# VectorE and the sync engine held to program order from the third batch on, with v split and loaded a head sooner and evenly shared heads

## The chip, the cores and the metric

The kernel runs on one core of one Trainium2 chip. The time is device microseconds (us) of one launch. Before the change three runs took 1080.21, 1080.63 and 1082.72 us, median 1080.63 us.

The core's engines work side by side, each through its own list of instructions from first to last: PE (TensorE, the matmuls; PEld are its weight loads), DVE (VectorE), ACT (ScalarE), POOL (GpSimd) and SP (the sync engine, which issues all DMAs here). An instruction waits on semaphores for what it needs from the other engines, and while it waits, whatever stands behind it on its own engine waits too.

## The reference

Attention with a decay, then a feed-forward layer with a hard swish. Shapes: q, k, v (8 batches, 8 heads, 576, 64), f (8, 8, 576), w_in (512, 2048), w_out (2048, 512).

```python
scores = scale * np.matmul(q, k.transpose(0, 1, 3, 2))
log_f = np.log(np.clip(f, 0.0001, 1.0))
cum = np.cumsum(log_f, axis=-1)
decay = cum[:, :, :, None] - cum[:, :, None, :]
scores = np.where(causal, -1000000000.0, scores + decay)
scores = scores - np.max(scores, axis=-1, keepdims=True)
attn = np.exp(scores)
attn = attn / (np.sum(attn, axis=-1, keepdims=True) + 1e-09)
x = np.matmul(attn, v)      # to (4608 tokens, 512)
h = x @ w_in
g = h * np.clip(h + 3.0, 0.0, 6.0) / 6.0
out = g @ w_out
```

## The kernel before

**Two streams of work.** The list `VH` holds the attention steps v = 0 to 67: four of kind A and eight of kind B (batch 0, in pieces), then one of kind F for each head n = 8 to 63 (v = n + 4; batch b = n // 8, head h = n % 8). The feed-forward layer works on nine tiles of 512 tokens. Tile t has 16 h units (`h_unit`, 12 matmuls each, then clip and product) and four out units (`out_unit`, 48 matmuls each). A loop over `VH` writes one attention step per pass and calls `fill(1)` eight times in it. Each call adds a rate to a credit, and as long as the credit is at least 1 it takes the next piece of a feed-forward unit from the list `units` (an h unit is two pieces of 1.05, an out unit eight of 0.95, a tile 64 in all). From the third batch on the rate is 1.02, so 8.16 per head. When the eight heads of a batch are done, `done` puts that batch's tile into `units`; after the last batch two tiles are left.

**One head of kind F** (`rows`) goes through two halves. PE makes the scores of a half (tile `pn`, lines 608 and 611: 8 matmuls for half 0, 4 for half 1). DVE adds the mask and takes the row maximum (line 619, three chunks in half 0 and two in half 1) and makes the bias `nb` (line 625). ACT takes the exponential (line 631) and casts it to 16 bits into a `ring` buffer (line 645). DVE makes the low part (line 648, two per half) and POOL the rest (lines 654, 659). SP transposes the ring buffer into `pT` by DMA (line 666). A pass later PE multiplies with v (`av`, tile `pav`, 40 matmuls), and DVE normalizes (`rs`, `xf`, lines 727 to 729; every second head `xhl`, line 735). Every second head SP transposes the result into `xT`, the feed-forward input (`x_move`, line 755).

**One h unit**: PE fills a PSUM bank `ph` with 12 matmuls (lines 781 to 783). ACT makes `r` from it in two segments, one for each batch that the tile touches (line 791). DVE multiplies (line 794), and this is the last read of the bank; ACT casts to `gT` (line 795) and DVE makes the low part (line 796). `mm_tile` has three such banks in turn, so the unit after next but one cannot start before line 794 of this one is done.

**v of a batch**: `load_v` loads it into `vst` (lines 359, 360; called at h = 6 of the batch before). `v_scale` (h = 7) finds its largest value with two reductions on DVE (line 365), a matmul `pt_v` and some small steps. `v_split` (lines 396, 397) makes 16-bit high and low parts for a pair of heads, at h = 7 for the first pair and at h = 1, 3 and 5 for the others.

**What sets the order.** The program is written once in this loop, but the order on each engine is decided by a scheduler that plays the program on a model of the chip and lets each engine take what is ready there, earlier lines first. So the lists of the engines are not in the program's order. [...]

Of the kernel before, what the change touches and what calls it, by code (L numbers as in the profile page):

```python
# [20 lines left out]
def kernel(  # L21
# [10 lines left out]
    nc = tc.nc  # L32
# [3 lines left out]
    B = vS.shape[0]  # L36
    H = NHEAD // B
    NT, DM = out.shape
    DFF = w_in.shape[1]
    P = 128  # L40
    NCH = 5
    CR = [128, 128, 128, 128, 64]
    SP = NCH * P
    NPAIR = H // 2
    NCC = DM // P
    NFC = DFF // P
    TT = 512
# [9 lines left out]
    ps_m = ctx.enter_context(tc.tile_pool(name="ps_m", bufs=2, space=bass.MemoryType.PSUM))  # L57
    ps_t = ctx.enter_context(tc.tile_pool(name="ps_t", bufs=1, space=bass.MemoryType.PSUM))
# [23 lines left out]
    NQK, NL, NST = 3, 2, 3  # L82
    W_RATE = (8, 5, 4)
    H_COST = 1.05
    F_RATE = (0.6, 0.45, 1.02)
    PIN = 0
    PIN0 = 1
    LOW_W = 0
# [6 lines left out]
    QA = 256  # L95
    CA = QA // P
    VH = [("A", g) for g in range(NPAIR)] + [("B", n) for n in range(H)]
# [54 lines left out]
    SV, IV, UO, UX, A1 = 0, 8, 16, 24, 32  # L152
# [25 lines left out]


    def pow2_scale(pm, s_col, i_col, name):  # L180
        pool, tag = (ps_t, "tr") if SV < s_col < SV + B else (ps_m, "mm")
        pt = pool.tile([P, 512], F32, tag=tag, name=f"pt_{name}")
        nc.tensor.matmul(pt[:, 0:1], ones, pm, start=True, stop=True)
        yield
        e = p2.tile([P, 2], F32, tag="ee", name=f"e_{name}")
        nc.vector.tensor_scalar(e[:, 0:1], pt[:, 0:1], 2.0 ** -100, None, op0=ALU.max)
        ei = e.bitcast(I32)
        nc.vector.tensor_scalar(
            ei[:, 1:2], ei[:, 0:1], 24, 23, op0=ALU.logical_shift_right, op1=ALU.logical_shift_left
        )  # L190
        si = SC.bitcast(I32)
        nc.vector.tensor_scalar(
            si[:, s_col:s_col + 1], ei[:, 1:2], -1.0, float(204 << 23), op0=ALU.mult, op1=ALU.add
        )
        nc.vector.tensor_scalar(
            si[:, i_col:i_col + 1], ei[:, 1:2], 1.0, float(50 << 23), op0=ALU.mult, op1=ALU.add
        )
        yield

    def scol(c):  # L200
        return SC[:, c:c + 1]
# [160 lines left out]
    def v_scale(b):  # L362
        pm = p2.tile([P, 2], F32, tag="pm", name=f"vm{b}")
        for i, t in enumerate(v_parts(b)):
            nc.vector.tensor_reduce(
                pm[:, i:i + 1], t.rearrange("p c (h e) -> p (c h) e", e=D + 1)[:, :, 0:D],
                axis=AX.XY, op=ALU.max, apply_absolute_value=True,
            )
            yield
        nc.vector.tensor_tensor(pm, pm, pm, op=ALU.mult)  # L370
        nc.vector.tensor_tensor(pm[:, 0:1], pm[:, 0:1], pm[:, 1:2], op=ALU.max)
        yield from pow2_scale(pm[:, 0:1], SV + b, IV + b, f"v{b}")
# [15 lines left out]
    def v_split(g):  # L388
        b, hp = divmod(g, NPAIR)
        t = v16[:, g % NV16]  # L390
        if g < NPAIR + NV16:
            nc.vector.memset(t[:, :, :, D:D + 1], 1.0)
        for j in range(2):
            o = (2 * hp + j) * (D + 1)
            src = vst[:, :, o:o + D]
            nc.scalar.activation(t[:, :, j, 0:D], src, AF.Copy, scale=scol(SV + b))
            nc.vector.scalar_tensor_tensor(
                t[:, :, j, D + 1:VW], src, scol(SV + b), t[:, :, j, 0:D],
                op0=ALU.mult, op1=ALU.subtract,
            )  # L400

    def load_x(v):
        kind, n = VH[v]
        t = ST[v % NST]
        if kind == "A":
            nc.sync.dma_start(
                t[:, 0:2 * QA].rearrange("p (h s) -> p h s", h=2),
                qk[2 * n:2 * n + 2, :, 0:QA].rearrange("h p s -> p h s"),
            )
        else:  # L410
            nc.sync.dma_start(t, qk[n])

    def load_c(v):
        kind, n = VH[v]
        t = TK[v % NQK].bitcast(F32)[D:D + 2]
        if kind != "A":
            nc.sync.dma_start(t[:, 0:S], scr[n])
            if kind == "F":
                nc.sync.dma_start(TQ[v % NQK].bitcast(F32)[D + 2:D + 4, 0:S], scr[n])
        elif n >= 2:  # L420
            nc.sync.dma_start(
                t[:, 0:2 * QA].rearrange("r (h s) -> r h s", h=2),
                scr[2 * n:2 * n + 2, :, 0:QA].rearrange("h r s -> r h s"),
            )
        else:
            for h in range(2):
                d = nc.sync.dma_start(
                    t[:, h * QA:(h + 1) * QA], cs.bitcast(F32)[2 * n + h:2 * n + h + 1, :, 0:QA]
                )
            if PIN0:  # L430
                small.append(d.ins)
# [386 lines left out]
    def moe_tile(t, c0=0, c1=TT):  # L818
        for fc in range(NFC):
            j, new = divmod(fc, NFC // NG)  # L820
            if new == 0 and t < B and c0 == 0:
                while j not in w_in_done:
                    next(w_in_q, None)
                moe_scale_in(t, j)
            yield from h_unit(t, fc, c0, c1)
        if t == 0:
            for _ in wq:
                pass
        if t < B and c0 == 0:
            moe_scale_out(t)  # L830
        for s in range(c0 // P, c1 // P):
            yield from out_unit(t, s)
# [43 lines left out]

    units = []

    credit, rates = [0.0], [1.0]

    def w_step():
        with tc.high_priority(offset=-LOW_W):
            next(wq, None)

    def fill(k):
        credit[0] += k * rates[0]
        while credit[0] >= 1 and units:
            with tc.high_priority(offset=-LOW_M):
                r = next(units[0], 0)
            if r == 0:  # L890
                units.pop(0)
            else:
                credit[0] -= r
        credit[0] = min(credit[0], 1.0)

    def one(*a):
        yield from moe_tile(*a)

    def done(v):
        kind, n = VH[v]  # L900
        if kind == "A":
            if n == NPAIR - 1:
                units.append(one(0, 0, QA))
            return
        b, h = divmod(n, H)
        if h == H - 1:
            units.append(one(b, QA if b == 0 else 0, TT))
            if b == B - 1:
                units.append(one(B))

    prev = None
    pend_x = None
    vq = v_scale(0)
    for i, (kind, n) in enumerate(VH):
        b, h = divmod(n, H)
        if kind == "A":
            b = h = 0
        wn = W_RATE["ABF".index(kind)]
        rates[0] = F_RATE[0] if kind == "B" else F_RATE[min(b, 2)]
        ahead = i + 2 < NV  # L920
        if i + 3 < NV:
            load_x(i + 3)
        if ahead:
            load_c(i + 2)
        if b + 1 < B and h == 6:
            load_v(b + 1)
        if b and h % 2 == 1 and h < H - 1:
            v_split((n + 1) // 2)
        sg = rows(i) if kind == "F" else scores(i)
        front = ahead and VH[i + 2][0] != "F"  # L930
        next(sg)
        if i + 1 < NV:
            rests(i + 1)
        if ahead:
            parts(i + 2)
        fill(1)
        if b + 1 < B and h == 7:
            vq = v_scale(b + 1)
        next(vq, None)
        fill(1)  # L940
        ph = next(sg)
        if i + 1 < NV and VH[i + 1][0] != "F":
            max_rows(i + 1)
        for _ in range(wn // 2):
            w_step()
        fill(1)
        next(vq, None)
        next(sg, None)
        fill(1)
        if pend_x is not None:  # L950
            x_move(pend_x)
            done(pend_x)
            pend_x = None
        if front:
            natural(i + 2, 0)
        fill(1)
        if b + 1 < B and h == 7:
            for _ in vq:
                pass
            if b:  # L960
                v_split((n + 1) // 2)
        for _ in range(wn - wn // 2):
            w_step()
        next(sg, None)
        fill(1)
        if front:
            natural(i + 2, 1)
        fill(1)
        if prev is not None:
            av(*prev)  # L970
            if VH[prev[0]][0] == "A" or VH[prev[0]][1] % 2 == 1:
                pend_x = prev[0]
        if n == H:
            v_split(n // 2)
        fill(1)
        prev = (i, ph)
    rates[0] = 1.0
    av(*prev)
    fill(4)
    x_move(prev[0])  # L980
    done(prev[0])
    while units:
        fill(1)


# [34 lines left out]
```

## Time and profile before

| | |
|---|---|
| time, median of 3 runs | 1080.63 us |
| the profiled execution: its time, its span | 1083.28 us, 1081.5 us |
| PE busy | 1010.1 us (93%) |
| DVE busy | 719.7 us (67%) |
| ACT busy | 610.1 us (56%) |
| POOL busy | 413.1 us (38%) |
| mean granted TensorE clock | 0.982 |

A line of a view names engine, source line, operation and tiles (out<-in). "Idle before" is the engine's idle time just before an instruction, with what ended it. Heads take some 13 us each in the middle of the run: head n = 16 starts its scores at 236.9 us, n = 35 at 499.2, n = 36 at 511.8, n = 43 at 608.6 and n = 44 at 621.1. After the last head (879.5 us) only feed-forward work is left.

### The profile page before, as it was taken

How to read it: one execution, taken by the hardware profiler on the slowest of the kernel's cores; microseconds unless marked ns; L12 is line 12 of the kernel's file. 1: busy time of each engine (PE TensorE's matmuls, PEld its weight loads, DVE VectorE, ACT ScalarE, POOL GpSimd, SP SyncE). 2: the span in 40 equal slices, each digit the busy share in tenths (PEclk: the TensorE clock that was granted, in tenths of full speed). 3: DMA queues.
4: the chain of work that ended last, by engine and by line, in shares of the span. 5: the costliest groups of instructions: out<-in, count | busy, mean ns of one | idle time of the engine just before them, and what ended most of it. 6: DMA issues, size and time to landing. Idle time of an engine off the chain costs nothing.

```text
span 1081.5 us, 20281 instructions
## 1 busy us (share of the span) xinstructions
PE 1010.1 (93%) x7074; PEld 577.4 (53%) x7074; DVE 719.7 (67%) x1887; ACT 610.1 (56%) x1285; POOL 413.1 (38%) x505
## 2 busy tenths in 40 slices
PE   2799977988999999999999989999999999999998
PEld 2567854755555555555555545555555555444443
DVE  7869899876885688468865795689668841510520
ACT  4778656845764577356754674477447841621520
POOL 7344455335434445444544444454445420000000
PEclk9989989999999999999999999999999999999999
DMA  8866547767756666667576856675666651000001
GB/s 258 277 172 194 150 105 134 179 127 150 156 114 141 140 146 118 137 129 164 108 139 138 164 113 130 146 166 114 128 140 128 106 112 46 1 10 30 1 1 39
DMA packets 261650, 133.74 MB, mean 124 GB/s; under 512 B 229444, under 2 KB 231036, under 8 KB 261548
## 3 DMA queue, kind: packets, MB, share of 16 engines
q1 hardware_dynamic: 261548, 132.45, 54.7%
q8 instruction: 56, 0.92, 0.3%
q14 instruction: 46, 0.38, 0.1%
HBM read 47.93 MB, written 9.73 MB: 53 GB/s over the span
## 4 chain that ended last, share of the span: by engine, by line
PE 64%; DVE 12%; DMA 9%; issue 5%; ACT 5%; SPq 2%; POOL 2%; DVEq 0%; POOLq 0%; ACTq 0%
PE po L803 10%; PE po L804 10%; PE po L805 10%; PE ph L781 7%; PE ph L782 7%; PE ph L783 7%; DMA vst<-in_vS_dram 3%; PE pn L611 3%; PE pn L608 2%; DVE pp L619 2%; DVE ring L648 2%; DMA T<-TK 1%; DVE gT L796 1%; DMA w<-in_w_in_dram 1%; DVE r L794 1%
## 5 line engine op out<-in xcount | busy, mean ns | idle before, releaser
L781 PE MATMUL ph<-xT,w 128*128 128x512 f16 (+1 forms) x640 | 231.2, 363 | 14.5 <-DVE r L794 9.1
L782 PE MATMUL ph<-xT,w 128*128 128x512 f16 (+1 forms) x640 | 230.2, 363 | 0.0
L783 PE MATMUL ph<-xT,w 128*128 128x512 f16 (+1 forms) x640 | 230.0, 363 | 0.0
L631 ACT ACTIVATE pp<-pp,nb 128x192 f32<-128x192 f32 x280 | 138.5, 552 | 148.8 <-DVE nb L625 145.8
L804 PE MATMUL po<-w,gT 128*128 128x512 f16 x576 | 216.3, 381 | 6.1 <-DVE w L294 6.1
L805 PE MATMUL po<-w,gT 128*128 128x512 f16 x576 | 215.9, 381 | 0.0
L803 PE MATMUL po<-w,gT 128*128 128x512 f16 x576 | 213.6, 381 | 1.1 <-ACT o L814 0.8
L648 DVE TENSOR_TENSOR ring<-pp,ring 128x128 f16<-128x128 f32 (+2 forms) x216 | 131.5, 622 | 84.1 <-ACT ring L645 83.2
L791 ACT ACTIVATE r<-ph,bias_r,SC 128x256 f32<-128x256 f32 (+7 forms) x272 | 144.4, 570 | 28.6 <-PE ph L783 27.9
L794 DVE SCALAR_TENSOR_TENSOR r<-r,ph 128x512 f32<-128x512 f32 (+1 forms) x160 | 100.1, 627 | 88.9 <-ACT r L791 88.6
L458 POOL TENSOR_TENSOR T<-ST,T 64x576 fp32r<-64x576 f32 (+1 forms) x68 | 101.2, 1488 | 143.2 <-DMA T<-TK 133.4
L619 DVE CUSTOM_DVE_ANT_0 pp<-pn,W 128x192 f32<-128x192 f32 x280 | 122.9, 482 | 20.6 <-PE pn L611 16.6
L796 DVE TENSOR_TENSOR gT<-r,gT 128x512 f16<-128x512 f32 (+1 forms) x160 | 118.3, 743 | 27.4 <-ACT gT L795 26.6
L795 ACT CAST gT<-r 128x512 f16<-128x512 f32 (+1 forms) x160 | 91.8, 575 | 75.9 <-DVE r L794 75.8
L608 PE MATMUL pn<-TK,TQ 68*128 68x192 f32 x336 | 124.1, 383 | 5.8 <-issue 5.0
L611 PE MATMUL pn<-T,T 128*128 128x192 f32 x336 | 113.5, 368 | 4.3 <-POOL T L458 4.3
L645 ACT CAST ring<-pp 128x192 f16<-128x192 f32 x280 | 112.9, 452 | 0.0
L455 POOL TENSOR_TENSOR T<-ST,TQ 64x576 fp32r<-64x576 f32 (+2 forms) x68 | 97.6, 1435 | 24.8 <-PE pn L611 18.2
L654 POOL TENSOR_TENSOR ring<-pp,ring 128x128 f16<-128x128 f32 x96 | 61.5, 641 | 105.5 <-ACT ring L645 83.7
L782 PEld LDWEIGHTS <-w 128*128 128x128 f16 x640 | 62.7, 99 | 65.8 <-issue 20.9
L805 PEld LDWEIGHTS <-gT 128*128 128x128 f16 x576 | 56.8, 99 | 74.9 <-issue 13.7
L781 PEld LDWEIGHTS <-w 128*128 128x128 f16 x640 | 63.1, 99 | 62.2 <-issue 14.3
(136 smaller groups left out, 1703.4 us busy)
## 6 DMA issues: line engine op xcount, KB each, us to landing
ST<-in_qk_dram SPq DMA_DIRECT2D x64, 288.0 KB
T<-TK SPq DMA_DIRECT2D x64, 144.0 KB
out_dram<-o SPq DMA_DIRECT2D x36, 256.0 KB
ring<-in_w_out_dram SPq DMA_DIRECT2D x16, 512.0 KB
T<-TQ SPq DMA_DIRECT2D x56, 144.0 KB
vst<-in_vS_dram SPq DMA_DIRECT2D x7, 1040.0 KB
ring<-in_w_in_dram SPq DMA_DIRECT2D x9, 512.0 KB
w<-in_w_in_dram SPq DMA_DIRECT2D x7, 512.0 KB
```

Source lines behind the costliest of these rows:

```text
L608: nc.tensor.matmul(dst, TQ[i][0:D + 4, qs], TK[i][0:D + 4, a:e], start=True, stop=False)
L611: nc.tensor.matmul(dst, T7[j][:, qs], T1[j][:, a:e], start=False, stop=True)
L619: nc.vector.tensor_tensor_reduce(pp[:r, w:w + kw], pn[:r, o:o + kw], W[:r, 4 * P + r - kw:4 * P + r], 1.0, -3.0e38, ALU.add, ALU.max, accu ...
L631: nc.scalar.activation(x_, x_, AF.Exp, bias=nb[:r, e0 + x:e0 + x + 1], scale=0.125)
L648: eng.tensor_tensor(hl[:r, a:a + c * P], pp[:r, at[c] + 64:at[c] + kw], hl[:r, h0[c] + 64:h0[c] + kw], op=ALU.subtract,)
L781: nc.tensor.matmul(ph, w1[0][:, cc, fs_], xh, start=(cc == 0), stop=False)
L782: nc.tensor.matmul(ph, w1[0][:, cc, fs_], xl, start=False, stop=False)
L783: nc.tensor.matmul(ph, w1[1][:, cc, fs_], xh, start=False, stop=(cc == NCC - 1))
L791: nc.scalar.activation(r[:, a:e], ph[:, a:e], AF.Relu, bias=bias_r, scale=scol(A1 + NG * b + fc * NG // NFC))
L803: nc.tensor.matmul(po, gT[:, 0, fc, ts_], w2[:, fc, 0, :], start=(fc == 0), stop=False)
L804: nc.tensor.matmul(po, gT[:, 0, fc, ts_], w2[:, fc, 1, :], start=False, stop=False)
L805: nc.tensor.matmul(po, gT[:, 1, fc, ts_], w2[:, fc, 0, :], start=False, stop=(fc == NFC - 1))
```

## The change

From the first head of batch 2 (n = 16, v = 20; that is the third batch) four things differ.

1. After the whole program is written, each DVE instruction from there on gets an order dependency on the DVE instruction written before it, and each SP instruction likewise. The scheduler can no longer reorder these two lists. PE, ACT and POOL are scheduled as before.
2. `v_split` for the pairs 2 and 3 of a batch comes at h = 2 and 4 (before: 3 and 5), ahead of `rows`; `load_v` comes at h = 5 (before: 6). `pt_v` takes one of the two `ps_m` banks, not the `ps_t` one.
3. The rate is what is left in `units`, less a reserve of 8, shared evenly over the passes up to h = 1 of the next batch, and held between 0.5 and 1.25.
4. `done` for an F batch comes one pass later than `x_move`, at the start of h = 2, and no longer right behind the transposes.

```diff
-    F_RATE = (0.6, 0.45, 1.02)
+    F_RATE = (0.6, 0.45)
+    IN_ORDER = ('DVE', 'SP')
...
-        pool, tag = (ps_t, "tr") if SV < s_col < SV + B else (ps_m, "mm")
+        pool, tag = (ps_t, "tr") if s_col == SV + 1 else (ps_m, "mm")
...
+    credit, rates, left = [0.0], [1.0], [0.0]
+    TILE = NFC * 2 * H_COST + TT // P * NFC // 2 * (2.0 - H_COST)
+    RESERVE = 8.0
+
+    def queue(unit, columns):
+        units.append(unit)
+        left[0] += TILE * columns / TT
+
+    def even(h):
+
+        heads = (1 - h) % H + 1
+        return min(max((left[0] - RESERVE) / (8 * heads), 0.5), 1.25)
...
+        if b == 1 and h in (1, 3, 5) or b > 1 and h in (1, 2, 4):
+            v_split(n // 2 + 1)
+        if b + 1 < B and h == (5 if b > 1 else 6):
             load_v(b + 1)
-        if b and h % 2 == 1 and h < H - 1:
-            v_split((n + 1) // 2)
+        if moved is not None:
+            done(moved)
+            moved = None
+        rates[0] = F_RATE[0] if kind == "B" else F_RATE[b] if b < 2 else even(h)
...
             x_move(pend_x)
-            done(pend_x)
+            if VH[pend_x][0] == "F":
+                moved = pend_x
+            else:
+                done(pend_x)
...
+    before = {}
+    for k, ins in enumerate(nc.cur_bb.bb.instructions):
+        name = str(ins.engine).split(".")[-1]
+        if name in IN_ORDER:
+            if k >= mark and name in before:
+                tc.add_manual_dep(
+                    ins, before[name],
+                    mybir.DependencyInfo(mybir.DependencyClass.NoSync, mybir.DependencyReason.DATA),
+                    reason="program order",
+                )
+            before[name] = ins.name
```

How the lists move, at three places. A source line of the changed kernel is one higher than before in this part (794 becomes 795). In a name the first number behind `pp`, `pn`, `nb`, `rs` or `xf` is v, and `r_3_10` is h unit 10 of tile 3.

**DVE, in the h units of tile 3, around the step v = 40 (n = 36).** Before:

```order
L625 TENSOR_SCALAR nb_40_6222<-MF0_108 128x2
L794 SCALAR_TENSOR_TENSOR r_3_10_0_6259<-r_3_10_0_6259,ph_3_10_0_6246 128x512
L648 TENSOR_TENSOR ring2_125<-pp_40_0_6232,ring2_125 128x128
L648 TENSOR_TENSOR ring2_125<-pp_40_0_6232,ring2_125 128x512
L794 SCALAR_TENSOR_TENSOR r_3_11_0_6298<-r_3_11_0_6298,ph_3_11_0_6274 128x512
L796 TENSOR_TENSOR gT_116<-r_3_10_0_6259,gT_116 128x512
L648 TENSOR_TENSOR ring0_123<-pp_40_1_6286,ring0_123 128x256
L648 TENSOR_TENSOR ring0_123<-pp_40_1_6286,ring0_123 128x384
L794 SCALAR_TENSOR_TENSOR r_3_12_0_6324<-r_3_12_0_6324,ph_3_12_0_6305 128x512
L727 TENSOR_SCALAR rs_39_1_6377<-pav_110 128x5
L796 TENSOR_TENSOR gT_116<-r_3_11_0_6298,gT_116 128x512
```

And now:

```order
L626 TENSOR_SCALAR nb_40_6110<-MF0_108 128x3
L376 SCALAR_TENSOR_TENSOR SC_120<-SC_120 128x1
L795 SCALAR_TENSOR_TENSOR r_3_4_0_6148<-r_3_4_0_6148,ph_3_4_0_6135 128x512
L797 TENSOR_TENSOR gT_116<-r_3_4_0_6148,gT_116 128x512
L649 TENSOR_TENSOR ring2_125<-pp_40_0_6120,ring2_125 128x128
L649 TENSOR_TENSOR ring2_125<-pp_40_0_6120,ring2_125 128x512
L620 ISA pp_40_1_6175,MF0_108<-pn_40_1_6170,W_88 128x320
L620 ISA MF0_108 128x1
L620 ISA pp_40_1_6175,MF0_108<-pn_40_1_6170,W_88 128x448
L620 ISA MF0_108 128x1
L626 TENSOR_SCALAR nb_40_6110<-MF0_108 128x2
L795 SCALAR_TENSOR_TENSOR r_3_5_0_6187<-r_3_5_0_6187,ph_3_5_0_6163 128x512
```

Before, other work stood between the product of a unit (line 794) and its low part (line 796), and the second half's maxima came ahead of the first half's low parts. Now the two steps of a unit stand next to each other, and half 1 (line 620 of `pp_40_1`) starts only behind the low parts of half 0.

**ACT, the list that serves this stretch now.** ACT itself is not held to program order, but its list is made around DVE's:

```order
L792 ACTIVATE r_3_6_0_6212<-ph_3_6_0_6199,bias_r_86,SC_120 128x192
L632 ACTIVATE pp_40_0_6120<-pp_40_0_6120,nb_40_6110 128x192
L632 ACTIVATE pp_40_0_6120<-pp_40_0_6120,nb_40_6110 128x576
L632 ACTIVATE pp_40_0_6120<-pp_40_0_6120,nb_40_6110 64x64
L792 ACTIVATE r_3_4_0_6148<-ph_3_4_0_6135,bias_r_86,SC_120 128x320
L792 ACTIVATE r_3_5_0_6187<-ph_3_5_0_6163,bias_r_86,SC_120 128x320
L792 ACTIVATE r_3_6_0_6212<-ph_3_6_0_6199,bias_r_86,SC_120 128x320
L646 CAST ring2_125<-pp_40_0_6120 128x192
L646 CAST ring2_125<-pp_40_0_6120 128x576
L646 CAST ring2_125<-pp_40_0_6120 64x64
L796 CAST gT_116<-r_3_4_0_6148 128x512
```

The second segment of unit 4 now stands behind the exponentials of `pp_40_0`, and unit 4's cast to `gT` behind two other units' segments and the casts of the ring.

**DVE, where v of batch 5 is scaled (`vm5`).** Before, in the step v = 39 (n = 35):

```order
L619 ISA pp_39_1_6104,MF1_109<-pn_39_1_6099,W_88 128x448
L619 ISA MF1_109 128x1
L365 TENSOR_REDUCE vm5_6760<-vst_112 128x1 x2
L648 TENSOR_TENSOR ring0_123<-pp_39_0_6050,ring0_123 128x128
L625 TENSOR_SCALAR nb_39_6040<-MF1_109 128x2
L796 TENSOR_TENSOR gT_116<-r_3_6_0_6077,gT_116 128x512
```

And now, in the step v = 43 (n = 39):

```order
L797 TENSOR_TENSOR gT_116<-r_3_15_0_6667,gT_116 128x512
L366 TENSOR_REDUCE vm5_6673<-vst_112 128x1
L649 TENSOR_TENSOR ring2_125<-pp_43_0_6647,ring2_125 128x128
L649 TENSOR_TENSOR ring2_125<-pp_43_0_6647,ring2_125 128x512
```

The reductions were pulled four steps ahead of where the program has them, between unit 6 and 7 of the tile; now they stand behind its last h unit, and two steps behind the load of `vst`, which SP issues in the step v = 41.

More of the change, by code (lines that the diff above doesn't have):

```diff
@@ L877 @@
     units = []
-    credit, rates = [0.0], [1.0]
+    credit, rates, left = [0.0], [1.0], [0.0]
[7 more added lines that the diff above has]
+        return min(max((left[0] - RESERVE) / (8 * heads), 0.5), 1.25)
     def w_step():
@@ L893, in fill @@
                 credit[0] -= r
+                left[0] -= r
         credit[0] = min(credit[0], 1.0)
@@ L902, in done @@
             if n == NPAIR - 1:
-                units.append(one(0, 0, QA))
+                queue(one(0, 0, QA), QA)
             return
@@ L906, in done @@
         if h == H - 1:
-            units.append(one(b, QA if b == 0 else 0, TT))
+            queue(one(b, QA if b == 0 else 0, TT), TT - QA if b == 0 else TT)
             if b == B - 1:
-                units.append(one(B))
+                queue(one(B), TT)
     prev = None
-    pend_x = None
+    pend_x = moved = None
     vq = v_scale(0)
@@ L918 @@
         wn = W_RATE["ABF".index(kind)]
-        rates[0] = F_RATE[0] if kind == "B" else F_RATE[min(b, 2)]
+        if b == 2 and h == 0:
+            mark = len(nc.cur_bb.bb.instructions)
         ahead = i + 2 < NV
@@ L924 @@
             load_c(i + 2)
-        if b + 1 < B and h == 6:
+        if b == 1 and h in (1, 3, 5) or b > 1 and h in (1, 2, 4):
+            v_split(n // 2 + 1)
+        if b + 1 < B and h == (5 if b > 1 else 6):
             load_v(b + 1)
-        if b and h % 2 == 1 and h < H - 1:
-            v_split((n + 1) // 2)
+        if moved is not None:
+            done(moved)
+            moved = None
+        rates[0] = F_RATE[0] if kind == "B" else F_RATE[b] if b < 2 else even(h)
         sg = rows(i) if kind == "F" else scores(i)
@@ L976 @@
         prev = (i, ph)
+    if moved is not None:
+        done(moved)
     rates[0] = 1.0
```

## The prediction

> **What bounds the kernel now.** I read the page first: the busy shares and the slices.
>
> ```profile
> PE 1010.1 (93%) x7074; PEld 577.4 (53%) x7074; DVE 719.7 (67%) x1887; ACT 610.1 (56%) x1285; POOL 413.1 (38%) x505
> PE   2799977988999999999999989999999999999998
> PEclk9989989999999999999999999999999999999999
> ```
>
> From the eleventh slice on (270 us) PE is at 9 tenths or more, up to the last slice. So in the part that the change touches (from n = 16 on, 236.9 us) time can be won only where PE still stands, and any new standing of PE is lost at full price. The next view is the waits of PE from 240 us to the end; columns are total us, times, longest.
>
> ```profile
> PE ph L781 <- DVE r L794: 8.1, 5, 3.2
> PE ph L781 <- DMA xT<-xhl: 5.3, 4, 2.2
> PE pav L691 <- DMA pT<-ring: 3.7, 2, 1.9
> PE po L803 <- ACT o L814: 0.8, 1, 0.8
> ```
>
> That is all: 17.9 us. The first row is PE waiting for a free `ph` bank. The timeline shows why, on SP, DVE and PE in turn:
>
> ```profile
> 612.45 0.83 SPq L359 DMA_DIRECT2D vst<-in_vS_dram  x1
> ```
> ```profile
> 621.22 2.88 DVE L365 TENSOR_REDUCE vm<-vst 128x1 f32<-128x1536 f32 x2 [4.16 <-DMA vst<-in_vS_dram]
> ```
> ```profile
> 403.75 0.38 PE L781 MATMUL ph<-xT,w 128*128 128x512 f16 x1 [2.17 <-DVE r L794]
> ```
> ```profile
> 626.22 0.41 PE L781 MATMUL ph<-xT,w 128*128 128x512 f16 x1 [3.23 <-DVE r L794]
> ```
>
> The reductions stand in DVE's list right behind the load of v. DVE waits 4.16 us for it, works 2.88 us on them, and PE runs out of banks. Such a stall costs a second time, in the granted clock. Windows (the last three columns are clock, DMA share, GB/s):
>
> ```profile
> 404.00:408.00 4.00, 4.00 (x13) 1.66 (x11) 3.97 (x12) 2.89 (x6) 0.91 (x1) 0.57 1.11 137
> 592.00:596.00 4.00, 3.32 (x43) 2.30 (x43) 2.54 (x7) 2.67 (x6) 0.80 (x1) 1.00 0.56 123
> 626.00:630.00 4.00, 3.78 (x10) 1.40 (x10) 3.97 (x14) 3.37 (x7) 1.12 (x2) 0.57 0.87 166
> ```
>
> Behind the stalls of 2.17 and 3.23 us the clock is 0.57 for 4 us, which is (1 - 0.57) x 4 = 1.7 us each; behind the longest wait for `xT` (2.2 us, ending at 592.7) it stays 1.00.
>
> **The change, part by part.**
>
> *v a head sooner, reductions in program order.* The load is now issued at h = 5 and the reductions come at h = 7, two heads or some 26 us later. In the rows above they ended their wait 621.22 - 612.45 = 8.8 us after the issue, so the wait goes. The 2.88 us of work stay, but behind the last h unit of the tile, where PE has out units that need no DVE; that work is the cover, and without it the 8.1 us would partly return. Gain: 8.1 + 2 x 1.7 = 11.5 us, at least 0. The `pt_v` bank moves to `ps_m`: it falls among the out units too, each of which holds its bank for 48 matmuls, so I put it at 0 (one unit, 2.6 us, at most).
>
> *Even shares, the reserve, `done` a pass later.* The transposes of `x_move` now have most of a head to land while 8 units (about a head's share) are still in hand. The 5.3 us for `xT` go. The queue ran dry in h = 1 of each batch at a rate of 8.16 a head against 64 a tile; now it does not. At the start (n = 16, 17) the rest of tile 0 is spread over two heads, which may take the 3.7 us for `pT` too; I count 0, and keep 3.7 for the range. Work moved past the last head is done there at the same price, since PE is full in both places: 0. SP in program order stands longer before single transfers, but what it brings is written a pass or more ahead: 0.
>
> *DVE in program order, in the h units.* Here the bill is made. A stretch of the last h units before the change without any stall of PE:
>
> ```profile
> 828.00:866.00 38.00, 38.00 (x290) 20.86 (x289) 33.57 (x85) 31.10 (x67) 18.07 (x22) 1.00 0.64 113
> ```
>
> PE 38.00 of 38, DVE 33.57, ACT 31.10: DVE has 4.4 us to spare in about 12 units and three heads, so 12.7 us a head with four units. What a unit costs DVE when its product and its low part stand next to each other is to be seen after the last head, where nothing else is in the list:
>
> ```profile
> 922.55 0.69 DVE L794 SCALAR_TENSOR_TENSOR r<-r,ph 128x512 f32<-128x512 f32 x1 [0.23 <-ACT r L791]
> 923.92 0.69 DVE L796 TENSOR_TENSOR gT<-r,gT 128x512 f16<-128x512 f32 x1 [0.69 <-ACT gT L795]
> ```
>
> DVE idles 0.69 us while ACT casts. The new list has this for every unit, and on ACT the cast often stands behind exponentials, ring casts and segments of later units. To price it I went through one stretch by hand: tile 3, the steps v = 39 to 42, with the lists shown with the change and these durations, first DVE, then ACT, then PE:
>
> ```profile
> 501.43 0.34 DVE L619 CUSTOM_DVE_ANT_0 pp<-pn,W 128x192 f32<-128x192 f32 x1
> 501.70 0.08 DVE L619 DVE_READ_ACCUMULATOR2_ANT MF<- 128x1 f32 x1
> 501.70 0.75 DVE L619 CUSTOM_DVE_ANT_0 pp<-pn,W 128x576 f32<-128x576 f32 x1
> 502.38 0.08 DVE L619 DVE_READ_ACCUMULATOR2_ANT MF<- 128x1 f32 x1
> 502.38 0.21 DVE L619 CUSTOM_DVE_ANT_0 pp<-pn,W 64x64 f32<-64x64 f32 x1
> 502.53 0.07 DVE L619 DVE_READ_ACCUMULATOR2_ANT MF<- 64x1 f32 x1
> 502.53 0.67 DVE L794 SCALAR_TENSOR_TENSOR r<-r,ph 128x512 f32<-128x512 f32 x1
> 503.13 0.81 DVE L735 TENSOR_TENSOR xhl<-xf,xhl 128x640 f16<-128x640 f32 x1
> ```
> ```profile
> 504.67 1.35 ACT L631 ACTIVATE pp<-pp,nb 128x192 f32<-128x192 f32 x3
> 505.92 0.34 ACT L645 CAST ring<-pp 128x192 f16<-128x192 f32 x1
> 506.16 0.62 ACT L795 CAST gT<-r 128x512 f16<-128x512 f32 x1
> 506.68 0.82 ACT L645 CAST ring<-pp 128x576 f16<-128x576 f32 x2
> 507.40 1.01 ACT L791 ACTIVATE r<-ph,bias_r,SC 128x192 f32<-128x192 f32 x2
> ```
> ```profile
> 514.58 0.38 PE L781 MATMUL ph<-xT,w 128*128 128x512 f16 x1 [0.94 <-DVE r L794]
> ...
> 516.95 0.38 PE L783 MATMUL ph<-xT,w 128*128 128x512 f16 x1
> ```
>
> So: maxima of half 0 take 1.1 us (501.43 to 502.53), a product or a low part 0.6 until the next may start and 0.7 until its result is there; three exponentials 1.25, a cast to `gT` 0.5 (0.6 until done), ring casts of a half about 1.0, a segment 0.5; a unit on PE 12 x 0.216 = 2.6 (twelve matmuls from 514.58 to 516.95). Half 1 (maxima, low parts) I scaled by columns to about 1.0 and 0.8, the 40 matmuls of `av` and the small steps to about 1.2 and 0.6, from 12.7 - 4 x 2.6 = 2.3 us of attention a head (with 3.0 the stalls below shrink by about a tenth).
>
> First head: PE fills three banks, then needs unit 0's back for unit 3. But DVE must first take the maxima (1.1), ACT the exponentials (1.3), only then unit 0's second segment (0.6), then DVE the product (0.7): with hand-overs 4.0 us behind the scores, while PE has 2.0 us of its own. **Stall 2.0**; the second half's scores then wait 0.85 more.
>
> The next two heads, in us from the end of the second half's scores of v = 40: DVE's low part of unit 3 ends at 7.1 (its cast stood behind unit 5's segment), v is split to 8.0, maxima 9.1, ACT exponentials 10.6, unit 4's segment 11.2, product 11.9: PE wanted that bank at 10.1 (**1.8**). ACT's segments and ring casts to 13.1, the cast of unit 4 at 13.7, its low part 14.3, the ring's low parts 15.1, maxima of half 1 at 16.1; PE wanted the score bank at 14.6 (**1.6**). Unit 5's product 16.8; exponentials and cast 17.9, low part 18.6, ring 19.4, unit 6's product 20.1 (**0.6**); low part 21.4, `xf` 22.0, `xhl` 23.6, maxima 24.7, unit 7's product 25.4 (**1.5**); unit 8's 29.3 (**1.2**). With 0.2 before: 6.9 us in two heads. The last third of the tile I put at 2.5, less than that rate. Sum for a tile 2.9 + 6.9 + 2.5 = 12.3 us; tiles 2 to 6: 61; tile 1, with (64 - 8) / 64 of the rate, 9. **Loss 70 us**; bounds 0 (all hand-overs fall into time that DVE had to spare) and 6 x 4.2 heads x 3.45 = 87 (every head like these two).
>
> *The clock.* The new stalls are 0.6 to 2.0 us; the row at 404 had 2.17 before it, the one at 592 none of it. I count three half-clock stretches, 3 x 1.7 = 5 us (0 to one in each of the 25 heads, 43).
> [...]
>
> **The sum.** The profiled execution took 1083.28 us: the span of 1081.5 and 1.8 around it. 1083.3 - 11.5 - 5.3 + 70 + 5 = 1141.5. The median of the three runs lies 2.65 below the profiled one, so **1139 us**.
>
> **Rivals.** *The order costs nothing (faster).* If ACT reaches the casts early enough that the 0.69 us fall where DVE waited before, only the gains remain: 1080.6 - 16.8 = 1064, with `pT` 1060, with half of them 1072. It speaks for it that DVE's waits of before (4.4 us in the 38) need not come on top. Against it: the hand-over alone is 12 x 0.69 = 8.3 us in that stretch, and more than 4.4. This decides: above 0.37 us of unhidden wait a unit (4.4 / 12) DVE is what PE waits for.
> *Only the bare hand-over counts (a little slower).* 8.3 - 4.4 = 3.9 us in 12 units, 5.2 in a tile, 31 in six: 1080.6 - 16.8 + 31 = 1095.
> *v stays late.* If the load, now held in SP's list, starts late, the reductions stand longer and 11.5 us stay: 1139 + 11 = 1150, inside the likeliest case's range.
>
> **Chances.** The likeliest, DVE and ACT hand each other the work and PE waits for both, 0.52, its own range 1110 to 1165. The bare hand-over, 1084 to 1110, 0.18. Faster, 1060 to 1077, 0.20. No change that a measurement of this kernel can tell (within 0.3%, 1077.4 to 1083.9), 0.05. Above 1165, by the clock, 0.05. The range from 1070 to 1165 leaves out the 0.05 above and some 0.12 of the faster case. Faster 0.20, same 0.05, slower 0.75.
>
> **What would show it.** In the changed kernel PE's wait for the product of `r` grows from 8.1 us to some 60 (with the waits for the maxima of `pp`), all while h units run; DVE's wait for the cast to `gT` becomes one of its largest; PE's slices there fall to 8 and below, and those with out units stay full. The reductions no longer wait for `vst`, and PE no longer for `xT`. I am wrong if PE stays full in the h units: then DVE's low parts will be seen to follow their products without the gap, or the gap where DVE had waited anyway.

## The result, and the profile after

The changed kernel takes **1244.9 us** (median of four runs, 1243.03 to 1249.91), the kernel before 1081.68 us in the same series: ratio 1.151 [1.146, 1.156]. Slower, as forecast, but by 163 us where 58 were forecast, and above the whole range. Times here and below are medians of the chip's usual, faster state; single slower executions (1298.7 us in e14, 2635.0 us in e18, 1096.4 us of the kernel before) are left out. The profiled execution has a span of 1241.2 us (before: 1081.5). Its page, busy shares, slices of PE and granted clock:

```profile
PE 1071.0 (86%) x7074; PEld 603.1 (49%) x7074; DVE 718.7 (58%) x1887; ACT 615.3 (50%) x1285; POOL 396.8 (32%) x505
PE   3799788878789778986799879978897889999998
PEclk9899989988899799998999899999999899999999
```

PE's slices fall to 6, 7 and 8 until the heads end (1050 us), as the prediction said. The clock row does not stay at 9 there any more; the prediction had counted on three short losses. The waits of PE from 240 us to the end (total us, times, longest):

```profile
PE pn L612 <- POOL T L459: 41.7, 26, 4.3
PE ph L782 <- DVE r L795: 31.4, 28, 4.1
PE pav L692 <- DMA pT<-ring: 19.2, 21, 1.9
PE ph L782 <- DMA xT<-xhl: 9.3, 5, 3.3
PE pn L609 <- DVE MF L620: 6.6, 6, 1.6
```

The product (31.4) and the maxima (6.6) make 38.0 us, less than the 60 foretold. The largest row is one that the prediction priced at nothing: PE waits for `T`, the part of q and k that GpSimd makes. The same stretch in windows, before and then after (length, busy us of PE, PEld, DVE, ACT and POOL, then clock, DMA share, GB/s):

```profile
240.00:1080.00 840.00, 819.85 (x5655) 435.08 (x5653) 516.75 (x1313) 452.50 (x950) 297.79 (x372) 0.99 0.52 108
```
```profile
240.00:1240.00 1000.00, 879.55 (x5661) 459.30 (x5659) 517.72 (x1330) 457.70 (x950) 283.03 (x373) 0.95 0.42 92
```

This splits the 160 us. PE stands 120.5 us where it stood 20.2 (+100), and it is busy 59.7 us longer with the same matmuls. By the granted clock, (1 - 0.95) x 1000 = 50 us are lost against (1 - 0.99) x 840 = 8, so some 42 of the 60 are the clock (the clock is given in hundredths, so this is good to some 9 us).

How it looks in one place: the two heads n = 36 and 37, in the stretch that the prediction priced by hand. They take 40.4 us, from 559.0 to 599.4, with seven h units in them. The window, and every stop of PE above 0.2 us:

```profile
558.96:599.40 40.44, 28.73 (x195) 15.13 (x192) 22.78 (x56) 19.23 (x41) 14.63 (x18) 0.92 0.39 79
```
```profile
560.42 0.38 PE L782 MATMUL ph<-xT,w 128*128 128x512 f16 x1 [1.08 <-DVE r L795]
564.56 0.36 PE L612 MATMUL pn<-T,T 128*128 128x192 f32 x1 [1.38 <-POOL T L459]
566.26 0.41 PE L609 MATMUL pn<-TK,TQ 68*128 68x320 f32 x1 [0.69 <-DVE MF L620]
571.23 0.39 PE L782 MATMUL ph<-xT,w 128*128 128x512 f16 x1 [1.38 <-DVE r L795]
578.42 0.20 PE L692 MATMUL pav<-v,pT 128*128 128x65 f16 x1 [1.62 <-DMA pT<-ring]
583.14 0.53 PE L612 MATMUL pn<-T,T 128*128 128x192 f32 x1 [3.36 <-POOL T L459]
594.46 0.39 PE L782 MATMUL ph<-xT,w 128*128 128x512 f16 x1 [1.43 <-DVE r L795]
598.05 0.20 PE L692 MATMUL pav<-v,pT 128*128 128x65 f16 x1 [0.61 <-DMA pT<-ring]
```

Product and maxima stop PE for 1.08 + 0.69 + 1.38 + 1.43 = 4.6 us; the hand-made chain had 6.9, for eight units. `T` adds 4.7, `pT` 2.2, and the clock of 0.92 another 3.2. So in these heads it was not the engine priced by hand that cost more than thought, but what lies around it.

One round of the loop, from 582 us on: the window, then the last matmul of a unit on PE, two rows of ACT and one of DVE.

```profile
582.00:590.00 8.00, 6.86 (x22) 3.84 (x23) 4.03 (x9) 0.69 (x2) 2.16 (x3) 0.57 0.28 53
```
```profile
589.33 0.38 PE L784 MATMUL ph<-xT,w 128*128 128x512 f16 x1
```
```profile
589.75 1.02 ACT L792 ACTIVATE r<-ph,bias_r,SC 128x192 f32<-128x192 f32 x2 [7.31 <-PE ph L784]
590.66 1.11 ACT L632 ACTIVATE pp<-pp,nb 128x320 f32<-128x320 f32 x2
591.67 0.61 ACT L796 CAST gT<-r 128x512 f16<-128x512 f32 x1
```
```profile
592.31 0.69 DVE L797 TENSOR_TENSOR gT<-r,gT 128x512 f16<-128x512 f32 x1 [5.78 <-ACT gT L796]
```

PE waited 3.36 us for `T` and then ran its unit at 0.57 of the clock. ACT idled 7.31 us, because a segment of that unit stands in its list ahead of the exponentials and of the cast of the unit before. DVE idled 5.78 us for that cast, and what stands behind it in its fixed line was late in turn.

### The profile page after: what moved, and what is told of

Read it like the earlier page. It is cut to its first block, busy times and chain, and to the rows that moved or that the text cites. A ratio compares the mean times of both kernels' runs of the same rounds, so it can differ in the third digit from the quotient of the medians.

```text
span 1241.2 us, 20253 instructions
## 1 busy us (share of the span) xinstructions
PE 1071.0 (86%) x7074; PEld 603.1 (49%) x7074; DVE 718.7 (58%) x1887; ACT 615.3 (50%) x1285; POOL 396.8 (32%) x505
## 4 chain that ended last, share of the span: by engine, by line
PE 39%; DVE 13%; DMA 12%; ACT 11%; SPq 9%; issue 8%; POOL 8%; POOLq 0%; ACTq 0%; DVEq 0%
PE po L804 6%; PE po L805 5%; PE po L806 5%; SPq L756 5%; PE ph L782 5%; PE ph L783 5%; PE ph L784 5%; DMA pT<-ring 4%; ACT pp L632 3%; DMA ST<-in_qk_dram 3%; POOL T L459 3%; DVE pp L620 3%; SPq L667 3%; DVE ring L649 3%; ACT r L792 2%
## 5 line engine op out<-in xcount | busy, mean ns | idle before, releaser
L782 PE MATMUL ph<-xT,w 128*128 128x512 f16 (+1 forms) x640 | 242.0, 378 | 42.7 <-DVE r L795 32.5
L783 PE MATMUL ph<-xT,w 128*128 128x512 f16 (+1 forms) x640 | 241.4, 378 | 0.0
L784 PE MATMUL ph<-xT,w 128*128 128x512 f16 (+1 forms) x640 | 239.4, 375 | 0.0
L649 DVE TENSOR_TENSOR ring<-pp,ring 128x128 f16<-128x128 f32 (+2 forms) x216 | 124.0, 598 | 83.7 <-ACT ring L646 82.8
L612 PE MATMUL pn<-T,T 128*128 128x192 f32 x336 | 103.8, 344 | 46.8 <-POOL T L459 46.7
L447 POOL TENSOR_SCALAR TK<-ST 64x576 fp32r<-64x576 f32 (+1 forms) x68 | 48.6, 715 | 268.5 <-DMA ST<-in_qk_dram 248.8
L620 DVE CUSTOM_DVE_ANT_0 pp<-pn,W 128x192 f32<-128x192 f32 x280 | 122.8, 482 | 19.2 <-PE pn L612 13.8
L609 PE MATMUL pn<-TK,TQ 68*128 68x192 f32 x336 | 113.3, 352 | 18.5 <-DVE MF L620 8.1
L782 PEld LDWEIGHTS <-w 128*128 128x128 f16 x640 | 65.2, 102 | 99.9 <-DVE r L795 28.6
L783 PEld LDWEIGHTS <-w 128*128 128x128 f16 x640 | 65.1, 102 | 79.2 <-issue 32.5
L784 PEld LDWEIGHTS <-w 128*128 128x128 f16 x640 | 65.3, 102 | 68.9 <-issue 13.8
```

Of the source, the lines that this page charges most:

```text
L620: nc.vector.tensor_tensor_reduce(pp[:r, w:w + kw], pn[:r, o:o + kw], W[:r, 4 * P + r - kw:4 * P + r], 1.0, -3.0e38, ALU.add, ALU.max, accu ...
L649: eng.tensor_tensor(hl[:r, a:a + c * P], pp[:r, at[c] + 64:at[c] + kw], hl[:r, h0[c] + 64:h0[c] + kw], op=ALU.subtract,)
L782: nc.tensor.matmul(ph, w1[0][:, cc, fs_], xh, start=(cc == 0), stop=False)
L783: nc.tensor.matmul(ph, w1[0][:, cc, fs_], xl, start=False, stop=False)
L784: nc.tensor.matmul(ph, w1[1][:, cc, fs_], xh, start=False, stop=(cc == NCC - 1))
```

## The experiments

Each run is compared with the kernel before in its own series (medians 1082 to 1085 us, so differences of 3 us between runs of different series say nothing). "Chained" means held to program order from the third batch on; line numbers of these kernels may be some lines higher.

| run | what is chained or changed | us | ratio to before |
|---|---|---|---|
| e3_free | nothing chained, all other parts of the change | 1098.2 | 1.012 [1.005, 1.020] |
| e2_sp_only | SP | 1153.5 | 1.063 [1.056, 1.069] |
| e8_sp_loads_free | SP, without the loads of q, k, decay | 1133.9 | 1.045 [1.041, 1.049] |
| e1_dve_only | DVE | 1237.3 | 1.142 [1.137, 1.146] |
| e7_dve_act | DVE and ACT | 1231.3 | 1.135 [1.130, 1.139] |
| e5_low_later | DVE, low parts written one unit later | 1150.7 | 1.058 [1.052, 1.065] |
| e6_max_free | DVE without maxima and bias | 1110.3 | 1.023 [1.018, 1.028] |
| e9_core | DVE's maxima, bias and products only | 1101.8 | 1.018 [1.015, 1.021] |
| e13_core_low | these and the low parts | 1101.9 | 1.013 [1.008, 1.019] |
| e14_core_ring | these (e9) and the ring's low parts | 1112.0 | 1.023 [1.017, 1.029] |
| e16_core_low_ring | e9 and both | 1169.2 | 1.080 [1.073, 1.087] |
| e18_all_but_v | e16 and the steps behind `av` | 1201.3 | 1.108 [1.100, 1.115] |
| e17_all_but_av | all of DVE but the steps behind `av` | 1159.8 | 1.070 [1.064, 1.076] |
| e12_both_freed | DVE without maxima, SP without loads and `T` transfers | 1120.8 | 1.035 [1.032, 1.039] |
| e4_old_ordered | kernel before with both chains | 1274.5 | 1.175 [1.170, 1.180] |
| e10_v_held | e3, v's reductions held in place | 1077.5 | 0.996 [0.993, 0.998] |
| e11_old_v_held | kernel before, v's reductions held | 1070.5 | 0.989 [0.985, 0.994] |
| e15_old_v_done | e11, next tile listed a pass later | 1066.2 | 0.980 [0.974, 0.986] |

**Which order costs?** e1 to e3 change one line, here that of e1; e4 adds the last block of the change to the kernel before.

```diff
-    IN_ORDER = ('DVE', 'SP')
+    IN_ORDER = ('DVE', )
```

> The changed kernel with only VectorE held to program order; the sync engine's list is free again. Theory H (hand-over: DVE and ACT hand each h unit to and fro, and that alone makes the loss): stays above 1200 us, PE waits for the product of r as in the changed kernel. Theory S (the sync engine's order makes most of it, because loads for later heads stand behind transposes that wait for the ring): back to 1100 to 1145, which is what the forecast priced for VectorE's order alone, and PE's wait for POOL's low parts (46.7 us in the changed kernel) is gone. Theory B (each order alone is bearable, the two together close a loop): 1070 to 1130.

> The changed kernel with only the sync engine held to program order; VectorE's list is free. Theory H: 1062 to 1080, as the forecast put the sync engine at 0. Theory S: above 1150, with PE waiting for POOL's low parts as in the changed kernel (46.7 us). Theory B: 1070 to 1130, less than half of the 163 us.

> The changed kernel with neither list held: only v a head sooner, even shares, the reserve, the later done and the bank of pt_v are left. All three theories put the loss into the order, so 1062 to 1082: at best the 17 us of PE waits for v and xT are won, at worst the scheduler pulls the reductions forward again as before and only the xT part (5 us) is. Above 1090 would mean that the shares or the later done cost something themselves.

> The kernel before, with both lists held to program order from the third batch on and nothing else. The order alone is then to cost what it costs in the changed kernel: 1235 to 1265 by all three theories, a little more than the changed kernel, since the waits for xT stay (5 us) and v is loaded one head before its reductions. Well under 1200 would mean that even shares or the moved v make the order dear.

Against e3, the chain on DVE costs 139 us, that on SP 55, both 147. So e1 came out as theory H has it and e2 as theory S: DVE's is the larger, SP's is far from free, and the two mostly replace each other. The other parts alone lose 16 us; e3 is above its range, and above the 1090 that was to mean that these parts cost something themselves. e4 is above its range too: in the kernel before the two chains cost 192 us, not 147, and PE waits 36.5 us for `xT` there, against 9.3 in the changed kernel, so the other parts do save something once the order is held. e1's waits of PE, its wait of DVE for the cast, and its window:

```profile
PE ph L782 <- DVE r L795: 63.2, 32, 6.8
PE pav L692 <- DMA pT<-ring: 34.0, 23, 4.1
PE pn L609 <- DVE MF L620: 12.0, 14, 1.8
```
```profile
DVE gT L797 <- ACT gT L796: 177.1, 128, 6.4
```
```profile
240.00:1230.00 990.00, 869.06 (x5660) 452.81 (x5658) 537.36 (x1332) 457.51 (x950) 291.21 (x372) 0.96 0.43 92
```

With DVE chained alone, product and maxima stop PE for 75.2 us, near the 70 foretold. But `pT` adds 34.0, and PE is busy 869.06 - 819.85 = 49 us longer than before.

In e3 the reductions of v are pulled forward again, and since the load now comes a head sooner, more than before. Its wait of DVE and of PE:

```profile
DVE vm L366 <- DMA vst<-in_vS_dram: 32.3, 5, 7.9
```
```profile
PE ph L782 <- DVE r L795: 23.8, 6, 6.8
```

**What in SP's line costs?** In e8 the calls of `load_x` and `load_c` are left out of the chain:

```diff
+            k0 = len(nc.cur_bb.bb.instructions)
             load_x(i + 3)
+            loose.update(range(k0, len(nc.cur_bb.bb.instructions)))
...
-        if name in IN_ORDER:
+        if name in IN_ORDER and k not in loose:
```

> SP alone in program order (1154 us so far), but the loads of q, k and the decay rows (ST, TK, TQ) are left out of the chain. Theory L (in the chain these loads stand behind transposes that wait for VectorE's ring parts, so GpSimd's TK waits 132 us for ST and PE waits 40 us for T): the wait of TK for ST goes, PE's wait for T falls below 12 us, and the time falls to 1095 to 1115. Theory X (the transposes themselves stand behind each other and behind the output stores): the time stays above 1135.

Neither theory holds whole: 20 of the 55 us go. In e2, SP's list and GpSimd's read so:

```profile
621.72 6.82 SPq L756 DMA_TRANSPOSE xT<-xhl  x5
628.65 2.71 SPq L667 DMA_TRANSPOSE pT<-ring  x1
631.40 0.59 SPq L412 DMA_DIRECT2D ST<-in_qk_dram  x1
```
```profile
634.68 0.67 POOL L447 TENSOR_SCALAR TK<-ST 64x576 fp32r<-64x576 f32 x1 [5.84 <-DMA ST<-in_qk_dram]
```

The load of q and k stands behind the transposes, and GpSimd waits for it. The kernel before has no such wait for `ST` after 240 us; e2 has 132 us of it, and e8 29.5. PE's wait for `T`, in e2 and in e8:

```profile
PE pn L612 <- POOL T L459: 40.4, 19, 4.2
```
```profile
PE pn L614 <- POOL T L459: 17.5, 15, 1.9
```

e8 keeps 36 us over e3. What they are (the `T` transfers, or the transposes behind each other) was not taken apart alone; GpSimd waits 155.2 us for a `T` transfer in e8 and 97.4 in e3, which speaks for the first.

**Is it the hand-over from product to low part?** e5 writes `low_part()` for the previous unit behind each product, e6 leaves the maxima out of the chain, e7 chains ACT as well.

```diff
         nc.vector.scalar_tensor_tensor(r, r, 6.0 * CG, ph, op0=ALU.min, op1=ALU.mult)
         nc.scalar.copy(gT[:, 0, fc, c0:c1], r)
-        nc.vector.tensor_tensor(gT[:, 1, fc, c0:c1], r, gT[:, 0, fc, c0:c1], op=ALU.subtract)
+        low_part()
+        lag.append((r, fc, c0, c1))
```

> VectorE alone in program order (1237 us so far), but each h unit's low part is written one unit later, right behind the next unit's product, so that VectorE no longer stands between product and low part while ACT casts. Theory H (the price is this hand-over, made once per unit): VectorE's wait for the gT cast falls from 143 us to under 30, and the time to 1100 to 1140. Theory M (the price is that score maxima and products stand in one fixed line, so a late exponential or segment on ACT holds both): the wait moves to the products or maxima, and the time stays above 1190.

> VectorE alone in program order, but the score maxima (pp) and their bias nb are left out of the chain, so the scheduler may put them anywhere; the hand-over between product and low part stays in every unit. Theory H: the hand-over still stands 96 times, so the time stays above 1190. Theory M: the maxima no longer hold or are held by products, and the time falls below 1140.

> VectorE and ACT both in program order. If ACT's free list is the amplifier (segments of later units stand ahead of exponentials and casts, so VectorE's waits get long), casts come right behind products: VectorE's mean wait for a gT cast falls from 1.5 us to about 0.7 (the bare hand-over) and the time falls from 1237 to 1150 to 1190. If the hand-over needs no amplifier, the time stays or rises, since ACT now has hand-overs of its own: 1230 to 1300.

e5 lies between the theories: 87 us go, 52 stay. DVE's wait for the cast to `gT` is gone in it, but its wait for the ring's casts grows from 76.1 us (e1) to 134.3. e6 came out as theory M has it. DVE's wait for the cast and PE's for the product in it:

```profile
DVE gT L801 <- ACT gT L800: 90.5, 89, 2.6
```
```profile
PE ph L786 <- DVE r L799: 18.5, 21, 2.4
```

Of the 90.5 us, 30.6 fall after the last head, where only feed-forward work is left (33.7 of the 177.1 in e1); among the heads 59.9 us remain of 143.5. So with the maxima free to overtake, DVE waits less for casts, and 127 of the 139 us go. But what remains does reach PE: it waits 18.5 us for the product here, and 0.8 us in e10 below, where nothing is held but v's reductions. The hand-over has a price of its own, a small part of the whole; the larger part is what it holds up. And e7 shows that the freedom of ACT's list is not the amplifier: in order, the casts are waited for just as long (177.4 us in 128).

**How much of the line is needed?** e9 chains only maxima, bias and products (the core); the next ones add to that.

```diff
+            core.update(range(k0, len(nc.cur_bb.bb.instructions)))
...
+        core.add(len(nc.cur_bb.bb.instructions))
         nc.vector.scalar_tensor_tensor(r, r, 6.0 * CG, ph, op0=ALU.min, op1=ALU.mult)
...
-        if name in IN_ORDER:
+        if name in IN_ORDER and k in core:
```

> Only score maxima, their bias and the products of the h units are chained on VectorE; everything else there, low parts included, and SP are free. Theory M1 (the fixed line of maxima and products alone is the price; who waits for casts does not matter): above 1190, as with all of VectorE chained (1237). Theory M2 (maxima cost only when they stand behind instructions that wait for ACT's casts, so both chain and hand-over are needed): 1098 to 1140, like the run without any chain (1098) and the one with later low parts (1151, which still has ring parts chained).

> The chain of maxima, bias and products (1102 us) plus the low parts of the h units; ring parts and all else free. If the low part's wait for its cast is what holds the maxima (theory M2, low parts): 1170 to 1230. If it is the ring's low parts that hold them: 1100 to 1120.

> The chain of maxima, bias and products (1102 us) plus the ring's low parts of VectorE; the h units' low parts are free. Ring parts come after the exponentials of their own half, so the maxima of the next half then wait for ACT's exponentials and ring casts of this one. If ring parts hold the maxima: 1140 to 1200. If low parts alone do: 1100 to 1120. The run with later low parts but all chained (1151) says that something beside them costs some 50.

> The chain of maxima, bias and products plus both the low parts of the h units and the ring's low parts; the steps behind av (rs, xf, xhl), v's steps and SP are free. Theory B (low parts and ring parts together make the line in which ACT and VectorE wait for each other in turn): 1170 to 1240. Theory V (the steps behind av, which wait for PE's 40 matmuls and these for a transpose, hold the line): 1105 to 1130.

> All of VectorE chained (1237 us) but the steps behind av (rs, xf, xhl). Theory V: 1110 to 1140. Theory B: 1200 to 1240. If v's steps hold the line as well: between.

> Maxima, bias, products, low parts, ring parts and the steps behind av chained; v's steps and the scales free. Theory V and theory B both: 1190 to 1240. If v's steps (the splits of v and its scale, five times a batch) hold the line: 1110 to 1150.

e9, at 1102, came out as theory M2 has it. Low parts add nothing to the core (1102 as well), ring parts 10, both together 67; the steps behind `av` another 32, and v's steps and scales the last 36. So neither the case of the low parts (1170 or more in e13) nor that of the ring parts (1140 or more in e14) came, and theory B holds for about half of the price: e16 stands at the lower edge of its range, e17 between its two theories, and e18 inside the range of both. In e13 DVE's wait for the cast, and PE's for the product; then the same and PE's for `pT` in e16:

```profile
DVE gT L803 <- ACT gT L801: 62.8, 83, 1.4
```
```profile
PE ph L786 <- DVE r L800: 8.7, 6, 3.4
```
```profile
DVE gT L806 <- ACT gT L804: 123.6, 112, 4.6
```
```profile
PE ph L789 <- DVE r L803: 35.8, 25, 3.4
PE pav L699 <- DMA pT<-ring: 29.4, 29, 3.9
```

My reading: as long as one kind of work that waits for ACT floats, it fills the time in which the other waits. That is argued from these rows, not shown by a run of its own. e17 and e18 agree: without the steps behind `av`, v's steps cost nothing on balance (1160 against 1169; with v in the line the 31 us of DVE's waits for `vst` are gone); with them they cost 36. Each link costs more the more of the others are there.

**Are these two things the whole price?**

> The changed kernel with both chains, but the score maxima and their bias are free of VectorE's, and the loads of q, k and decay and the T transfers free of SP's. If these two are the whole price (1245 against 1098 without chains): 1100 to 1125. If the chained transposes or the handing over of low parts cost something of their own: 1140 to 1180.

1120.8, inside the first range: with the maxima out of DVE's chain, and loads and `T` transfers out of SP's, 124 of the 147 us that both chains cost against e3 are gone. That range was set against e3, though, which pays for early reductions of v that this kernel does not have (next runs). Against e10 43 us of 167 stay, with 20.4 us of PE's waits for the product and 17.6 for `pT`; so the two are most of the price, and not the whole.

**What do the other parts bring without the order?** e10 ties the reductions to the score maxima written before them (in e3), e11 to the DVE instruction written before them (in the kernel before). Here that of e11:

```diff
+            if k in held:
+                tc.add_manual_dep(
+                    ins, before['DVE'],
+                    mybir.DependencyInfo(mybir.DependencyClass.NoSync, mybir.DependencyReason.DATA),
+                    reason="program order",
+                )
```

> The changed kernel without chains (1098 so far), but the two reductions of v from the third batch on must stand behind the score maxima written before them. If the early reductions (32 us of VectorE's waits for vst, 24 us of PE's for the product) are what the other parts lose: VectorE's wait for vst goes, PE's wait for the product falls below 8 us, and the time to 1068 to 1082. If the loss lies in the shares or the moved pieces: it stays at 1090 to 1100.

> The kernel before with one thing added: the reductions of v from the third batch on keep their place behind the VectorE instruction written before them. Its wait for vst (some 4 us a batch) goes; PE's 8.1 us for the product and the half clock behind two of them go: 1068 to 1077. If the list's order put them there because nothing else could use the time, the 2.9 us of work stall PE elsewhere: within 3 us of the kernel before.

> The kernel before with v's reductions held in place (1071 us) and, from the third batch on, the next tile put into the list one pass after its transposes. If its remaining 6.0 us of PE's waits for xT go with that: 1063 to 1067. If the queue of feed-forward work runs dry in the meantime and PE stands elsewhere: 1070 to 1080.

e10, e11 and e15 came out within their first ranges. In e11 PE's wait for the product is down from 8.1 to 0.2 us; what remains is this:

```profile
PE ph L785 <- DMA xT<-xhl: 6.0, 3, 2.7
```

e15 takes the next tile into the list a pass later, and that wait falls to 2.4 us. **1066.2 us, ratio 0.980 [0.974, 0.986]: the fastest version.** By medians it is 16 us ahead of the 1082 us of the series of e11, and 19 ahead of the 1085 of its own. e10, which has the even shares and the earlier splits too, stays at 0.996; one row of its PE waits is the `pt_v` step, priced at 0 in the prediction:

```profile
PE pt_v L184 <- DVE vm L375: 4.4, 4, 1.8
```

e10 also bears on the sums above. e3's early reductions cost it 21 us (1098.2 to 1077.5). Kernels whose DVE line holds v's steps (e1, e5, e6, e7, e12, e17) have no wait for `vst` after 240 us, so against e3 a gain of this size hides part of what their order costs. Against e10 all of DVE's line costs 160 us, not 139, and the line without the maxima (e6) 33, not 12.

## Why the prediction was wrong

The forecast of 58 us was 57 of standing of PE (70 - 8.1 - 5.3) and 2 of clock (5 - 3.4); the trace has 100 of standing and 60 of slower work. So the terms that failed are the clock's 5 us and, in the standing, the 0 for SP and the missing term for `pT`. One after the other:

*Gains, 11.5 for v and 5.3 for `xT`: right, but only without the rest.* e11 gains 1082.2 - 1070.5 = 11.7 us, and e15 16 to 22 us (by medians, or by its ratio) where 16.8 were foretold, with PE waiting only 4.7 us for the product, `xT` and `pT` after 240 us (17.1 before). In the changed kernel the waits for `vst` and the product behind them are gone as foretold (DVE's wait for the cast, 176.2 us, is its largest there, also as foretold), but PE's wait for `xT` is 9.3 us, not 0.

*Even shares and moved work, priced at 0: wrong.* e10 has both gains and is 11 us behind e15 by medians, 17 by ratios, so they, with `pt_v` and the earlier splits, cost about that much. Which of them was not tried apart.

*The order of DVE, "Loss 70 us": the sum of these waits was about right, the loss was not.* Where DVE alone is chained, product and maxima stop PE for 75.2 us. That it comes so near 70 is partly luck: it is 46 stops of up to 6.8 us where stalls of 0.6 to 2.0 were foreseen, tile 1 was put at 9 us where 56/64 of 12.3 are 10.8, and in the changed kernel, for which the 70 stood, it is 38.0. The step left out what else comes late with DVE's line: the ring's low parts release SP's transposes, these release `av`, and so PE waits 34.0 us for `pT` (3.7 before). The prediction looked only at the banks and has no term for the growth of that wait.

*The reason behind it: right as a sign, wrong as a size.* The prediction's deciding point was 0.37 us of unhidden hand-over per unit. Among the heads there are 96 units, and DVE waits for their casts 143.5 us in e1, 59.9 in e6 and 27.2 in e13: 1.5, 0.6 and 0.3 a unit. e1 and e6 are past the point and lose 160 and 33 us against e10; e13 is short of it and loses 4 against e3. So the rival "the order costs nothing" is about right for e13, the one of the bare hand-over (31 us) near what e6 loses, which may be chance, and both are far off for the full line. What the point does not give is what the wait holds up: the maxima standing behind it make most of the price, and low parts, ring parts and the steps behind `av` cost more together than each alone.

*The clock, 5 us: the step that failed worst.* I counted three stretches of half clock, because stalls of 0.6 to 2.0 us had seemed harmless. In the trace's clock records from 240 us to the last matmul there are 21 (96 us in all) where there were 3 (14 us), so 48 us are lost against 7, 41 more, close to the 42 from the windows. My own upper bound, 43, was about what came; it was left out of the range with a chance of 0.05. About 20 us of the 60 by which PE is busy longer are left unexplained by it.

*SP, priced at 0: wrong by 55 us alone.* "Written a pass or more ahead" was looked at for the order in the program, not for what stands in the queue ahead of a load: transposes that wait for DVE's ring parts. In the changed kernel SP's 41.7 us for `T` stand largely in place of DVE's (75.2 become 38.0, `pT` 34.0 become 19.2), so beside the chain on DVE it adds only 8 us.

*A line misread.* PE's slices before are not all at 9 from the eleventh on: the 24th (622 to 649 us) is at 8, with the stall of 3.23 us in it. The sum had that stall, so nothing follows from it.

## What to carry to other kernels

Before an in-order line is priced, list for each instruction that waits not only its own wait but what stands behind it and which engine needs that; here freeing the maxima alone gave back 127 us. Compare such a line with a kernel that has its side gains without it, or they hide part of the price. A reordering scheduler's one bad choice was best mended where it was: two instructions a batch held in place and one call moved gained some 2%, while holding all of both lists lost 15%. And where PE starts to stop often for a microsecond or more, give the clock a term of its own: here some 41 us beside 100 us of stops.

## What the hardware showed that I had not expected

Stops of PE well under 2 us were followed by half the clock: 1.42, 1.52 and 1.14 us, then 0.50. All three are in the changed kernel, with no other stop of more than 0.2 us in the 3.4 us ahead of the loss; two of them, and the windows behind all three:

```profile
280.24 0.36 PE L612 MATMUL pn<-T,T 128*128 128x192 f32 x1 [1.42 <-POOL T L459]
```
```profile
295.12 0.41 PE L609 MATMUL pn<-TK,TQ 68*128 68x320 f32 x1 [1.52 <-DVE MF L620]
```
```profile
282.10:285.50 3.40, 3.40 (x10) 1.22 (x8) 2.05 (x5) 0.62 (x1) 2.18 (x2) 0.50 0.00 0
295.76:299.16 3.40, 3.40 (x10) 1.16 (x9) 1.62 (x4) 2.68 (x6) 2.03 (x3) 0.50 0.72 136
1002.31:1005.71 3.40, 3.40 (x10) 1.21 (x8) 1.83 (x5) 0.94 (x3) 1.28 (x2) 0.50 0.23 46
```

The third followed a stop of 1.14 us. In the changed kernel 12 of the 13 stops above 2 us were followed by half clock and the other fell into it, and 10 of the 37 between 1 and 2 us were; in e1 it was 12 of 21 above 2 us, and one of 2.90 us was not. The stretches last 3.41 us or two or four times that, and start on multiples of it from each other (268.44, 282.09, 295.75 us). So in these traces it seems to depend on where a stop falls in a running window of 3.41 us.

The trace bears that out when it is cut into such windows from these starts. In the window before each of the 21 losses of the changed kernel PE stood for 1.28 us or more in sum, and every window at full clock in which it stood for more than 1.62 us was followed by a loss; in e1, with 19 losses, the two figures are 1.52 and 2.02. So in these traces the sum of the stops in a window tells more than the longest of them.
